# Row maxima of the verdict, gate weights and filler matmuls of the front put at other places in the engines' orders of a gated recurrence with a dense mixture of experts

## The chip, the cores and the metric

The kernel runs on one core of one Trainium2 chip. That core has TensorE (PE in the profile, its weight loads PEld), VectorE (DVE), ScalarE (ACT), GpSimd (POOL), SyncE (SP, which here only issues DMAs) and 16 DMA engines. Each engine runs its own list of instructions in order and waits at an instruction until what it needs is there. The metric is the time of one execution in microseconds (us).

## The reference

Two stages. A gated linear recurrence in each of 4 x 8 heads makes x, 3072 tokens by 384; a dense mixture of 8 experts (384 to 1024 to 384) is applied to x, each expert's result weighted with a column of P, which eight rounds of row and column normalization (Sinkhorn) make from the gate's logits.

```
f = 1 / (1 + exp(-f_logit))
for t in range(S):                       # S = 768, head_dim 48
    state = f[t] * state + outer(k[t], v[t])
    y[t] = q[t] @ state
x = y as (3072, 384)
P = exp(x @ w_gate - max); 8 x: P /= P.sum(1); P /= P.sum(0); P *= N / E
out = sum over e of P[:, e] * (relu(x @ w1[e]) @ w2[e])
```

## The kernel before

All values are float32. A product is made from float16 pairs: each operand is split into a high and a low part (names ending in h and l: ACT makes the high part, DVE the low one as the difference), and TensorE adds three products, hh, hl and lh.

**The front and the items.** The recurrence is cut into 24 items. An item loads q, k and f as one tile (q_1 for item 1; its DMA is line 493) and v (vr, line 498). ACT makes the gates ft (line 502), DVE scans them (r, line 507, then pi, its reciprocal, and the scaled q), splits keys and queries (kb line 551, ql line 554), TensorE transposes the keys (ktp, drained by ACT into kt, line 533), makes the scores (aps, masked by DVE as am, line 571) and the block states (kvps; u, st and sl on DVE, lines 582, 583 and 593), and then the item's result (yps of the item), which ACT and DVE drain as xh (line 616) and xl (line 619). Then the gate of an item, `gate` at line 472, multiplies x by the gate weights wgs into lps. The first three items are written as `early_item` (line 487), the others as `item`. Each is a generator that is moved on by one step per turn of the loop at lines 895 to 911; g counts the turns.

**Filler.** While items run, the first two experts are already computed on the tokens that are ready. `moe_tile` (line 404) does one expert on 128 tokens: 36 + 36 first-layer matmuls (hps, made into hh and hl), then 24 second-layer matmuls (yps_0_0 for the first tile), drained by ACT into yr_0_0 and stored. `fill` (line 845) issues as many matmuls of this filler per turn as the table FILL (line 80) gives credits: an entry (g, n) gives n credits from turn g on; a first-layer matmul of the first tiles costs a third of a credit, a second-layer one a whole.

**Loads.** `load` (line 335) brings a quarter of an expert's w1 or w2: a DMA into w1r or w2r, then ACT makes w1h or w2h (line 347), then DVE w1l or w2l (line 349), each at its own step. `first` is the list of the eight loads of expert 0 (four w1, then four w2). `gate_weights` (line 313) has the DMA of wgr and, one step later, one ACT and one DVE instruction that make wgs. `at_steps` puts a step of such a load into a turn.

**Order.** `mm` (line 278) hangs every matmul behind the one written before it, and `pin` (line 270) does the same for an engine's other instructions; so the order in the code is the order on TensorE, ACT, DVE and POOL. All matmuls have line 279 in the profile. DMAs are issued on SP.

**The second stage.** 48 periods (`period`, line 1198) do the other six experts on larger tiles. Each has 15 slots of six first-layer matmuls (kb_A to kb_F, drained by ACT and DVE), and between them the second-layer matmuls of the period before (`layer2`, line 1066): groups of twelve into a PSUM tile kyps, which is added to acc by DVE (line 1089) or by ACT (yt, line 1092) and POOL. The pool `psm` that kyps comes from has two buffers. In some of the last periods a chain of checks runs at given slots. Its end is `verdict` (line 799), which brings five columns of 128 numbers down to one number each: `partition_reduce` (line 94) transposes a column on TensorE into a tile gd_t of the same pool `psm`, and DVE reduces the row (gd_r, line 99). Between the two is a `yield`, so that the reduce comes in the chain's next slot. The numbers only decide whether a general path is used instead, which these inputs don't take.

## Time and profile before

| | |
|---|---|
| median of 3 runs | 1570.53 us (1569.91 to 1571.93) |
| profiled execution | 1571.4 us |
| its span, first to last instruction | 1569.7 us |
| mean granted TensorE clock | 0.994 |
| moved by DMA | 114.39 MB, 73 GB/s |

The profile is one execution. Busy times are sums over instructions; the chain that ended last is followed back from the last instruction through what released each. A wait is put down to the instruction that came last. In rows of the timeline the first two numbers are the start and the length in us, and what is in brackets is the idle time just ahead on that engine and what ended it.

### The profile page before, as it was taken

What the parts mean: (1) busy time and instruction counts of PE and PEld (TensorE: products, weight loads), DVE (VectorE), ACT (ScalarE), POOL (GpSimd) and SP (SyncE); (2) the same over time, 40 slices, a digit from 0 to 9 for tenths busy, and PEclk for the clock granted to TensorE, in tenths of its full rate; (3) what the DMA queues carried; (4) which work ended last, traced back from release to release, by engine and by line L of the source; (5) the groups of instructions that cost most, each with busy time, mean ns of one, the idle gap of its engine ahead of it and who ended that gap; (6) DMA issues with size and microseconds to landing.
All of it is one profiled execution on the core that took longest, in us unless ns stands there. A gap on an engine that the chain in (4) does not pass through costs nothing.

```text
span 1569.7 us, 32490 instructions
## 1 busy us (share of the span) xinstructions
PE 1527.5 (97%) x13462; PEld 1108.9 (71%) x13462; DVE 1095.0 (70%) x1810; ACT 778.2 (50%) x1489; POOL 515.2 (33%) x656
## 2 busy tenths in 40 slices
PE   7799999999999999999999999999999999999998
PEld 4588887666555777777777777777777777776675
DVE  7878888895776766676767677666666666755554
ACT  5555556553333655555455554445444445444432
POOL 1144444453529112333333332223322223222211
PEclk8999999999999999999999999999999999999999
DMA  8265445541001222232322222121212111100011
GB/s 254 74 147 140 121 121 132 135 116 35 20 27 50 67 63 79 66 92 66 91 66 84 74 86 62 47 65 42 68 44 63 42 43 51 32 11 11 6 51 69
DMA packets 89678, 114.39 MB, mean 73 GB/s; under 512 B 50640, under 2 KB 67152, under 8 KB 89520
## 3 DMA queue, kind: packets, MB, share of 16 engines
q1 hardware_dynamic: 89520, 112.22, 25.5%
q8 instruction: 107, 1.75, 0.5%
q14 instruction: 51, 0.42, 0.1%
HBM read 88.41 MB, written 14.16 MB: 65 GB/s over the span
## 4 chain that ended last, share of the span: by engine, by line
PE 89%; DVE 5%; ACT 2%; DMA 1%; POOL 1%; issue 1%; SPq 0%; ACTq 0%; DVEq 0%; POOLq 0%
PE kyps L279 35%; PE yps L279 12%; PE hps L279 10%; PE kb_B L279 8%; PE kb_A L279 8%; PE kb_D L279 6%; PE kb_C L279 4%; PE kb_E L279 2%; PE kb_F L279 2%; PE kvps L279 1%; PE aps L279 1%; DMA q<-in_qkf_dram 1%; POOL xs L936 1%; DVE hl L381 1%; DMA w1r<-in_w_dram 0%
## 5 line engine op out<-in xcount | busy, mean ns | idle before, releaser
L1093 POOL TENSOR_TENSOR acc<-acc,yt 128x384 f32<-128x384 f32 x172 | 173.3, 1008 | 638.0 <-ACT yt L1092 638.0
L279 PE MATMUL kyps<-k2h,kh 128*128 128x384 f16 x1152 | 375.5, 326 | 5.8 <-ACT yt L1092 2.1
L279 PE MATMUL kyps<-k2l,kh 128*128 128x384 f16 x1152 | 375.5, 326 | 0.0
L279 PE MATMUL kyps<-k2h,kl 128*128 128x384 f16 x1152 | 375.5, 326 | 0.0
L279 PEld LDWEIGHTS <-k1h 128*128 128x128 f16 x2880 | 281.5, 98 | 70.5
L279 PEld LDWEIGHTS <-kh 128*128 128x128 f16 x2304 | 225.4, 98 | 103.8
L1092 ACT ACTIVATE yt<-kyps,pes 128x384 f32<-128x384 f32 x172 | 100.1, 582 | 325.8 <-PE kyps L279 323.9
L279 PEld LDWEIGHTS <-k1l 128*128 128x128 f16 x1440 | 140.7, 98 | 63.2 <-issue 7.5
L1089 DVE SCALAR_TENSOR_TENSOR acc<-kyps,pes,acc 128x384 f32<-128x384 f32 x92 | 56.8, 618 | 175.3 <-PE kyps L279 175.3
L279 PEld LDWEIGHTS <-kl 128*128 128x128 f16 x1152 | 112.7, 98 | 53.1 <-issue 9.0
L279 PE MATMUL yps<-w2h,hl 128*128 128x384 f16 x384 | 125.9, 328 | 4.5 <-DVE hl L428 4.5
L1186 ACT ACTIVATE cp<-kb_A 128x512 f32<-128x512 f32 x144 | 86.3, 599 | 85.6 <-PE kb_A L279 85.0
L279 PE MATMUL yps<-w2l,hh 128*128 128x384 f16 x384 | 125.9, 328 | 1.5 <-DVE w2l L349 1.5
L279 PE MATMUL yps<-w2h,hh 128*128 128x384 f16 x384 | 125.7, 327 | 0.2 <-DVE hl L381 0.2
L279 PEld LDWEIGHTS <-w1h 128*128 128x128 f16 x1344 | 99.5, 100 | 33.9 <-issue 3.0
L1186 ACT ACTIVATE cp<-kb_B 128x512 f32<-128x512 f32 x144 | 87.2, 605 | 52.6 <-DVE kb_B L1188 51.0
L1191 DVE TENSOR_TENSOR cp<-kb_D,cp 128x512 f32<-128x512 f32 x144 | 98.8, 686 | 16.2 <-PE kb_D L279 15.3
L279 PEld LDWEIGHTS <-hh 128*128 128x128 f16 x768 | 74.8, 99 | 47.1 <-issue 2.6
L279 PE MATMUL hps<-xl,w1h 128*128 128x128 f16 (+1 forms) x672 | 86.0, 260 | 1.5 <-DVE xl L619 1.1
L279 PE MATMUL hps<-xh,w1h 128*128 128x128 f16 (+1 forms) x672 | 85.1, 260 | 0.5 <-DVE hl L381 0.4
L279 PE MATMUL hps<-xh,w1l 128*128 128x128 f16 (+1 forms) x672 | 85.1, 260 | 0.0
L279 PE MATMUL kb_A<-xbh,k1h 128*128 128x256 f16 x288 | 78.5, 273 | 0.2 <-ACT cp L1186 0.2
(243 smaller groups left out, 3616.6 us busy)
## 6 DMA issues: line engine op xcount, KB each, us to landing
wm<-in_w_dram SPq DMA_DIRECT2D x64, 384.0 KB, 3.0
q<-in_qkf_dram SPq DMA_DIRECT2D x23, 672.0 KB, 5.2
vr<-in_vbd_dram SPq DMA_DIRECT2D x24, 384.0 KB, 3.5
ys<-yr SPq DMA_DIRECT2D x48, 192.0 KB, 2.3
k1r<-in_w_dram SPq DMA_DIRECT2D x24, 384.0 KB, 3.0
k2r<-in_w_dram SPq DMA_DIRECT2D x24, 384.0 KB, 3.1
yb<-ys SPq DMA_DIRECT2D x48, 192.0 KB, 2.4
out_dram<-acc SPq DMA_DIRECT2D x24, 192.0 KB, 1.9
```

Of the source, the lines that this page charges most:

```text
L279: ins = (nc.tensor.transpose if transpose else nc.tensor.matmul)(**kw)
L381: held[0] = pin(nc.vector.scalar_tensor_tensor(out=tl, in0=ps, scalar=0.0, in1=th, op0=ALU.max, op1=ALU.subtract))
L936: pin(nc.gpsimd.tensor_tensor(out=block(r), in0=block(p), in1=block(q), op=ALU.add if op == '+' else ALU.subtract))
L1089: pin(nc.vector.scalar_tensor_tensor(out=y, in0=ps, scalar=p, in1=y, op0=ALU.mult, op1=ALU.add))
L1092: pin(nc.scalar.activation(out=yt, in_=ps, func=AF.Copy, scale=p))
L1093: pin(nc.gpsimd.tensor_tensor(out=y, in0=y, in1=yt, op=ALU.add))
L1186: pin(nc.scalar.activation(out=fresh(ev[2]), in_=bk, func=AF.Copy))
L1191: pin(nc.vector.tensor_tensor(out=fresh(ev[4]), in0=bk, in1=old, op=ALU.add if ev[2] == '+' else ALU.subtract))
```

## The change

Two parts.

1. `partition_reduce` has no `yield` any more: the row's reduce is issued right behind its transpose, in the same slot; `verdict` then yields twice after each column, so that the transposes stay in their slots.
2. In the front, the credits of turns 4 to 7 are spread: six second-layer matmuls of the first tile in each of turns 5, 7, 8 and 10. The DMA of wgr is issued ahead of those of w1r, and wgs is made ahead of the first xh. The four loads of w2r are issued behind item 1's q and v. w1h_2 is made behind the first xh, w1l_2 ahead of item 1's r, and the w2h and w2l come later.

```diff
-FILL = ((0, 12), (1, 8), (2, 4), (3, 0), (4, 6), (8, 0), (12, 4.7), (22, 8.7), (43, 8.2))
+FILL = ((0, 12), (1, 8), (2, 4), (3, 0), (5, 6), (6, 0), (7, 6), (9, 0), (10, 6), (11, 0), (12, 4.7), (22, 8.7), (43, 8.2))
...
     row = pool.tile([1, 1], F32, name=name + "_r")
-    yield
     pin(nc.vector.tensor_reduce(out=row, in_=ps[0:1, :], axis=AX.X, op=op))
     return row
...
         for n, (col, op) in enumerate(((5, ALU.min), (4, ALU.max), (2, ALU.max), (6, ALU.min), (0, ALU.min))):
-            rows.append((yield from partition_reduce(nc, cst, psm, "m", identf, g[:, col:col + 1], op, f"gd{n}", mm, pin)))
+            rows.append(partition_reduce(nc, cst, psm, "m", identf, g[:, col:col + 1], op, f"gd{n}", mm, pin))
+            yield
             yield
...
     wgen = gate_weights()
     it = early_item(0)
     go(it)
-    for gen in first:
+    go(wgen)
+    for gen in first[:4]:
         go(gen)
     nxt = early_item(1)
     go(nxt)
-    go(wgen)
+    for gen in first[4:]:
+        go(gen)
     go(it, 8)
     go(first[0])
     go(it, 2)
     go(first[1])
     go(it)
     go(first[0])
+    go(wgen)
+    go(it)
     go(it)
     go(first[2])
-    go(it)
     go(first[3])
     go(it)
     go(nxt)
     go(first[1])
+    go(first[2])
     live, g = [it, nxt], 0
     for n in range(2, 8):
-        at_steps(first[n], *((n - 2,) if n < 4 else (n - 2, n - 1)))
-    at_steps(wgen, 11)
+        at_steps(first[n], *((0,), (1,), (2, 3), (3, 5), (5, 7), (6, 10))[n - 2])
```

What this moves on the engines is shown at three places. Lines of the changed kernel are one lower than before up to the loop and three higher behind it. A row has line, operation, what is written, what is read and the shape; the number at the end of a name tells one tile from another.

SP at the start of the program, before: the loads behind item 0's.

```order
L498 DMA vr_161<-in_vbd_dram 128x768
L343 DMA w1r_0_163<-in_w_dram 128x768
L343 DMA w1r_1_165<-in_w_dram 128x768
L343 DMA w1r_2_167<-in_w_dram 128x768
L343 DMA w1r_3_169<-in_w_dram 128x768
L343 DMA w2r_0_171<-in_w_dram 128x768
L343 DMA w2r_1_173<-in_w_dram 128x768
L343 DMA w2r_2_175<-in_w_dram 128x768
L343 DMA w2r_3_177<-in_w_dram 128x768
L493 DMA q_1_179<-in_qkf_dram 112x1536
L498 DMA vr_181<-in_vbd_dram 128x768
L315 DMA wgr<-in_wg_dram 128x384
```

The same place in the changed kernel:

```order
L497 DMA vr_161<-in_vbd_dram 128x768
L314 DMA wgr<-in_wg_dram 128x384
L342 DMA w1r_0_165<-in_w_dram 128x768
L342 DMA w1r_1_167<-in_w_dram 128x768
L342 DMA w1r_2_169<-in_w_dram 128x768
L342 DMA w1r_3_171<-in_w_dram 128x768
L492 DMA q_1_173<-in_qkf_dram 112x1536
L497 DMA vr_175<-in_vbd_dram 128x768
L342 DMA w2r_0_177<-in_w_dram 128x768
L342 DMA w2r_1_179<-in_w_dram 128x768
L342 DMA w2r_2_181<-in_w_dram 128x768
L342 DMA w2r_3_183<-in_w_dram 128x768
```

q_1 and vr of item 1 have gone ahead of the four w2r, and wgr ahead of everything but item 0's own loads.

DVE in the front, before: item 1 from its split of the keys (kb) to its masked scores (am) and its first state (u), and then to the last piece before xl.

```order
L551 TENSOR_TENSOR kb_125<-q_1_179,kb_125 48x8x64 x2
L349 SCALAR_TENSOR_TENSOR w2l_1_510<-w2r_1_173,w2h_1_509 128x768
L554 TENSOR_TENSOR ql_499<-q_1_179,qh_498 112x512
L349 SCALAR_TENSOR_TENSOR w2l_2_520<-w2r_2_175,w2h_2_519 128x768
L564 SCALAR_TENSOR_TENSOR vl_139<-vr_181,vh_133 128x768
L349 SCALAR_TENSOR_TENSOR w2l_3_565<-w2r_3_177,w2h_3_564 128x768
L571 SCALAR_TENSOR_TENSOR am_589<-aps_538,mask 128x512
L582 TENSOR_TENSOR u_1_618<-kvps_0_594,st_576 112x384
```

In the changed kernel:

```order
L550 TENSOR_TENSOR kb_125<-q_1_173,kb_125 48x8x64 x2
L553 TENSOR_TENSOR ql_501<-q_1_173,qh_500 112x512
L348 SCALAR_TENSOR_TENSOR w2l_1_512<-w2r_1_179,w2h_1_511 128x768
L563 SCALAR_TENSOR_TENSOR vl_139<-vr_175,vh_133 128x768
L570 SCALAR_TENSOR_TENSOR am_577<-aps_529,mask 128x512
L348 SCALAR_TENSOR_TENSOR w2l_2_556<-w2r_2_181,w2h_2_555 128x768
L581 TENSOR_TENSOR u_1_604<-kvps_0_582,st_568 112x384
```

w2l_1 stands behind ql now, w2l_2 behind am, and w2l_3 has left this place: it comes behind item 2's r, pi and reciprocal, ahead of the carry. On TensorE the first six second-layer matmuls, which stood ahead of ktp_1_0, stand behind aps; only these six are ahead of kvps_0, where eighteen were; and the last six stand behind item 1's own yps and a wps.

DVE in the second stage, before: the slots at and behind the first of the five transposes (acc is the add of a kyps group, kb_A to kb_D are drains of the first layer).

```order
L1188 TENSOR_TENSOR kb_A<-kb_A,cp_13_19170 128x512
L1089 SCALAR_TENSOR_TENSOR acc_8534<-kyps_0_1_19178,pes,acc_8534 128x384
L994 SCALAR_TENSOR_TENSOR k1l_2_18993<-k1s_2_18900,k1h_2_18992 128x640 x2
L1188 TENSOR_TENSOR kb_B<-kb_B,cp_0_19231 128x512
L1089 SCALAR_TENSOR_TENSOR acc_8534<-kyps_1_0_19220,pes,acc_8534 128x384
L994 SCALAR_TENSOR_TENSOR k1l_2_18993<-k1r_2_18865,k1h_2_18992 128x256
L994 SCALAR_TENSOR_TENSOR k1l_2_18993<-k1r_2_18865,k1h_2_18992 128x384
L1188 TENSOR_TENSOR kb_C<-kb_C,cp_9_19260 128x512
L1191 TENSOR_TENSOR cp_2_19277<-kb_D,cp_6_19203 128x512
L1196 SCALAR_TENSOR_TENSOR kl_0_0_19119<-kb_A,kh_0_0_19118 128x512
L1188 TENSOR_TENSOR kb_D<-kb_D,cp_7_19294 128x512
L99 TENSOR_REDUCE gd_r<-gd_t 1x1
```

In the changed kernel:

```order
L1191 TENSOR_TENSOR kb_A<-kb_A,cp_13_19170 128x512
L98 TENSOR_REDUCE gd_r<-gd_t 1x1
L1092 SCALAR_TENSOR_TENSOR acc_8534<-kyps_0_1_19178,pes,acc_8534 128x384
L997 SCALAR_TENSOR_TENSOR k1l_2_18993<-k1s_2_18900,k1h_2_18992 128x640 x2
L1191 TENSOR_TENSOR kb_B<-kb_B,cp_0_19232 128x512
```

The reduce has moved up by ten instructions, from behind the drain of kb_D to just behind that of kb_A. The other four move in the same way.

## The prediction

> **What bounds the kernel now.** I read the page's shares first, then the list of waits on TensorE, then the stretches in which those waits lie.

> ```profile
> PE 1527.5 (97%) x13462; PEld 1108.9 (71%) x13462; DVE 1095.0 (70%) x1810; ACT 778.2 (50%) x1489; POOL 515.2 (33%) x656
> PE 89%; DVE 5%; ACT 2%; DMA 1%; POOL 1%; issue 1%; SPq 0%; ACTq 0%; DVEq 0%; POOLq 0%
> ```

> TensorE is busy for 97% of the span and carries 89% of the chain that ends last. No matmul is removed, so only time in which TensorE waits can be won. The list of waits on TensorE (engine and line waited for, us in total, times, longest) has these entries where the change works:

> ```profile
> PE lps L279 <- DVE wgs L318: 3.3, 1, 3.3
> PE aps L279 <- DVE ql L554: 2.9, 2, 1.6
> PE kvps L279 <- ACT kt L533: 2.4, 1, 2.4
> PE kyps L279 <- ACT yt L1092: 2.1, 3, 0.7
> PE kyps L279 <- DVE acc L1089: 2.1, 3, 0.7
> PE yps L279 <- DVE w2l L349: 1.5, 1, 1.5
> PE ktp L279 <- DVE kb L551: 0.5, 1, 0.5
> ```

> They lie in two places: the front (before 55 us: wgs, ql, kt, w2l, kb) and the five periods of the second stage in which the verdict transposes a column (acc, yt).

> **The verdict.** Six successive periods, one undisturbed and then the five with a transpose (start:end, length, busy time of PE, PEld, DVE, ACT, POOL, granted clock, DMA share, GB/s):

> ```profile
> 1368.19:1389.79 21.60, 21.60 (x164) 15.84 (x162) 13.44 (x35) 10.89 (x21) 8.26 (x14) 1.00 0.04 13
> 1389.79:1412.74 22.95, 22.11 (x165) 15.91 (x163) 13.83 (x24) 9.12 (x17) 3.99 (x4) 1.00 0.07 18
> 1412.74:1436.42 23.68, 22.22 (x166) 15.91 (x164) 12.52 (x22) 11.81 (x22) 8.24 (x14) 1.00 0.06 18
> 1436.42:1459.96 23.54, 22.18 (x164) 15.91 (x163) 14.79 (x27) 10.06 (x18) 3.99 (x4) 1.00 0.00 1
> 1459.96:1483.70 23.74, 22.40 (x165) 15.90 (x163) 11.85 (x22) 9.33 (x17) 3.98 (x4) 1.00 0.01 1
> 1483.70:1506.65 22.95, 22.11 (x165) 15.91 (x163) 11.06 (x19) 9.11 (x17) 4.00 (x4) 1.00 0.12 42
> ```

> The five are 22.95 + 23.68 + 23.54 + 23.74 + 22.95 = 116.86 us long, where five of the undisturbed length are 108.00: an excess of 8.86 us. Its cause stands in the rows of the transposed column and its reduce, and in TensorE's timeline:

> ```profile
> L279 PE MATMUL gd_t<-identf,wg x5: 272/272/273, 1394.7 to 1488.6; 128*1 128x128 f32 x5
> L99 DVE TENSOR_REDUCE gd_r<-gd_t x5: 267/268/269, 1407.3 to 1501.2; 1x1 f32<-1x128 f32 x5
> ...
> 1401.04 0.33 PE L279 MATMUL kyps<-k2l,kh 128*128 128x384 f16 x1
> 1402.08 0.32 PE L279 MATMUL kyps<-k2h,kh 128*128 128x384 f16 x1 [0.71 <-DVE acc L1089]
> ```

> The first column is transposed at 1394.7 and reduced at 1407.3. For 12.6 us, over half a period, it holds one of the pool's two PSUM buffers, and the groups of second-layer matmuls (kyps) share the other: each can begin only when the group before has been drained by its add. The timeline shows one such start, 1.04 us behind the matmul before it, though nothing else stood between.

> The change puts the reduce into the slot of the transpose. DVE is busy for 11 to 15 us of these periods, so it has room, and no instruction is added: a reduce of 0.27 us stands earlier. The buffer is then free long before the next group asks for it, as in the undisturbed period. What stays is the five transposes themselves on TensorE: between nothing (hidden) and their 0.272 us each (1.36 in all); two matmuls of 256 columns in the neighbourhood are 0.11 us apart, and I take that, 5 × 0.11 = 0.55. **The verdict's term is −(8.86 − 0.55) = −8.3 us**, between −7.5 and −8.86. The new cost, DVE waiting at the reduce for the transpose with the add of a kyps group behind it, is at least nothing and at most a transpose and a reduce, 0.54 us each time; it is DVE's and not TensorE's time, and DVE's idle hours cover it (22.95 − 13.83 = 9.1 us in the first of the periods), so I take nothing. If that cover were gone, 5 × 0.54 = 2.7 us would come back.

> **The front.** From lps on (the gate of item 0) all engines have the same order in both kernels, so the term of the front is how much earlier the first-layer matmuls of item 1's tile begin, just behind lps. They stand here now, with the instructions that lead there (start, us, engine, line, operation, idle time before it and what ended it):

> ```profile
> 5.05 3.76 SPq L343 DMA_DIRECT2D w2r<-in_w_dram  x4
> 10.44 0.33 SPq L498 DMA_DIRECT2D vr<-in_vbd_dram  x1
> ...
> vr<-in_vbd_dram SPq DMA_DIRECT2D x3, 384.0 KB, 12.4
> ...
> 17.07 0.85 ACT L347 ACTIVATE w1h<-w1r 128x768 f16<-128x768 f32 x1
> 21.20 0.62 ACT L502 ACTIVATE ft<-q 112x504 f32<-112x504 f32 x1 [3.29 <-DMA q<-in_qkf_dram]
> 40.31 0.49 ACT L442 ACTIVATE yr<-yps 128x384 f32<-128x384 f32 x1 [2.23 <-PE yps L279]
> 43.02 1.32 ACT L616 ACTIVATE xh<-yps 96x384 f16<-96x384 f32 x4 [0.62 <-PE yps L279]
> 46.53 0.53 ACT L317 ACTIVATE wgs<-wgr 128x384 f16<-128x384 f32 x1
> ...
> 18.60 0.96 DVE L349 SCALAR_TENSOR_TENSOR w1l<-w1r,w1h 128x768 f16<-128x768 f32 x1
> 21.86 1.23 DVE L507 TENSOR_TENSOR_SCAN r<-ft,ind 112x512 f32<-112x512 f32 x1 [2.31 <-ACT ft L502]
> 28.76 0.69 DVE L428 SCALAR_TENSOR_TENSOR hl<-hps,hh 128x512 f16<-128x512 f32 x1 [0.61 <-ACT hh L427]
> 33.52 0.69 DVE L554 TENSOR_TENSOR ql<-q,qh 112x512 f16<-112x512 f32 x1
> 35.86 0.95 DVE L349 SCALAR_TENSOR_TENSOR w2l<-w2r,w2h 128x768 f16<-128x768 f32 x1
> 36.72 0.69 DVE L571 SCALAR_TENSOR_TENSOR am<-aps,mask 128x512 f32<-128x512 f32 x1
> 39.41 0.56 DVE L582 TENSOR_TENSOR u<-kvps,st 112x384 f32<-112x384 f32 x1 [1.99 <-PE kvps L279]
> 41.56 0.96 DVE L593 SCALAR_TENSOR_TENSOR sl<-st,sh 112x768 f16<-112x768 f32 x1 [0.41 <-ACT sh L587]
> 44.02 0.51 DVE L544 TENSOR_TENSOR carry<-kvps,st 112x384 f32<-112x384 f32 x1
> ...
> 47.33 0.25 PE L279 MATMUL lps<-wgs,xh 128*128 128x16 f16 x3 [3.28 <-DVE wgs L318]
> 47.52 1.44 PE L279 MATMUL hps<-xh,w1h 128*128 128x128 f16 x12
> ```

> A w2l takes 35.86 to 36.72 = 0.86 us of DVE, and I use 0.87. I walk down this list with the new order.

> *Loads.* q_1 now goes ahead of the four w2r instead of behind them, so ft no longer waits 3.29 us for it; what ends last then is ACT's w1h work. With w1h_2 now behind the first xh, two w1h stand before ft: 17.07 + 2 × 0.79 = 18.65 instead of 21.20. The price is on the w2r. The last of the loads, vr_1, landed at 10.44 + 12.4 = 22.8; the same set now ends with w2r_3, behind one more load, wgr. So w2r_3 lands near 23.7 and w2r_0 before that; ACT asks for w2h_0 near 24.5. I cost it at nothing; each us later than that would cost up to one.

> *DVE to ql.* r comes behind two w1l: 18.60 + 2 × 0.87 = 20.35, 1.5 us earlier. kt, kvps, hps and hh follow ft (2.55 us earlier) and I let them move by 2.4, a little less, since TensorE has item 0's matmuls to end first; hl, which waits for hh, is at 26.35 (−2.4). From hl to ql DVE needed 33.52 − 28.76 = 4.76 us. In it w2l_1 (0.87) and an idle 0.43 before it go, since w2l_1 now stands behind ql: 3.45 remain, and ql starts at 29.8 (−3.7).

> *am, u, sl.* Between ql and am DVE has now w2l_1 and vl, not three pieces of w2l and vl: am at 29.8 + 0.6 + 2 × 0.87 = 32.15 (−4.6). u waited 1.99 us because twelve second-layer matmuls stood ahead of kvps_0 on TensorE at half rate. Now six stand there: aps ends near 31.2, six by 0.16 to 0.32 are 1 to 1.9 us, kvps takes 0.7, so it is ready at 32.9 to 33.8, while DVE is free at 32.15 + 0.61 + 0.87 = 33.65. I take u at 33.8 (−5.6) and sl, the same 2.15 us behind, at 35.95, ending at 36.9 (−5.6).

> *What is late next.* Item 1's yps could be drained into xh at about 37.4. But the last six second-layer matmuls need w2l_3, which now stands behind r, pi and the reciprocal on DVE, and yr_0_0 stands ahead of xh on ACT. From sl's start to the carry were 44.02 − 41.56 = 2.46 us, so w2l_3 runs from 38.4 to 39.3, the six matmuls end at 40.3, yr takes 0.4 and 0.5 us with its start, and xh runs from 40.85 to 42.15. Some 3.4 us of the gain are given back here. The wait for wgs, 3.28 us, is gone: its ACT instruction (0.53 us) now lies in ACT's wait for the first xh, and its DVE one ahead of the first xl. Were it not hidden there, ft would end at 18.65 + 0.53 + 0.62 = 19.8, still ahead of r at 20.35.

> So hps begins at 42.25 instead of 47.52: **the front's term is −5.3 us.** All listed stalls of the front together, 3.28 + 1.6 + 2.43 + 1.5 + 0.5 = 9.3 us, are its upper end; the lower end is nothing, if DVE's work after it swallows what is won.

> Against the profiled execution (span 1569.7 us, run 1571.4) the sum is −8.3 − 5.3 = −13.6, or 1557.8. Its run lies 0.9 us above the median of 1570.53; I give the forecast against the median: **1556.9 us.**

> One more thing speaks for caution, the clock that TensorE was granted in two stretches of the front (columns as above):

> ```profile
> 28.40:35.20 6.80, 3.24 (x40) 1.86 (x39) 6.00 (x9) 5.37 (x10) 0.38 (x1) 1.00 0.44 137
> 35.20:38.60 3.40, 3.40 (x14) 1.75 (x12) 2.21 (x3) 0.63 (x1) 0.00 (x0) 0.50 0.97 305
> ```

> Behind 6.8 us in which TensorE was busy for 3.24, the next 3.4 us ran at half rate. The change takes the second-layer matmuls out of the wait for kb: from the end of wps (25 to 27) to kb's end at 29.8 TensorE has nothing to do. A stretch of 3.4 us at half rate costs at most 1.7 us.

> [...]

> **The rivals.** 0.2% of this kernel, 3.1 us, is about what a measurement of it can tell from no change.

> - *One more stretch at half clock* in the front, as above, with no other one saved: 1556.9 + 1.7 = 1558.6. For it speaks the new wait; against it that the kernel already ran at half rate in 35.2 to 38.6 and would only exchange one such stretch for another.
> - *The front gives nothing*: DVE is the bound there, and what TensorE no longer waits for at lps it waits for later: 1570.5 − 8.3 = 1562.2. Against it: DVE's own instructions ahead of lps end five us earlier too.
> - *The front gives all its stalls*: 1570.5 − 8.3 − 9.3 = 1552.9. Against it: the 3.4 us given back at yr.
> - *The verdict gives nothing*: the buffers do not alternate again, because the reduce still ends too late for the group that wants its buffer. 1570.5 − 5.3 = 1565.2. Against it: the reduce is now 0.3 us behind the transpose, and a slot is 21.60 / 15 = 1.44 us.
> - *It does not do what it says*, each wait being replaced by one of equal length: 1570.5.
> - *Slower*: the w2r land late. On ACT w2h_0 stands ahead of hh_0_0_1, qh and vh, so each us past 24.5 delays item 1 by one. The verdict's 8.3 and the front's 5.3 cover 13.6 us; to be slower by 3.1 it needs 16.7 us, a landing after 41 us, while the whole set ended at 22.8; 1574 at that point.

> **How the numbers follow.** The forecast of 1556.9 has 0.55; half clock (1558.6) 0.15; front nothing (1562.2) 0.10; front all (1552.9) 0.08; verdict nothing (1565.2) 0.07; no effect (1570.5) 0.03; slower (1574) 0.02. Faster by over 0.2% hold all but the last two: 0.95, within 0.2% 0.03, slower 0.02. The range runs from all stalls of the front, 1552.9, to none of them, 1562.3.

> **What would show it.** In the profile after: the five periods with a transpose at about 21.7 us each, reduces within a us of their transposes, no wait of kyps on acc or yt there; ft at 18.6, ql at 29.8, sl at 36, yr just ahead of xh at 40.9, no wait for wgs, lps near 42.2. I would be wrong if ft still waited for q_1, if ACT waited for w2r, if the periods kept over 22.5 us, or if the time from lps to the second stage grew by what the front won.

## The result, and the profile after

| | before | changed |
|---|---|---|
| median | 1571.10 us (4 runs, 1569.91 to 1571.93) | 1560.88 us (4 runs, 1560.01 to 1561.55) |
| span of the profiled execution | 1569.7 us | 1558.3 us |

The ratio is 0.9935, with a 95% interval from 0.9918 to 0.9952: 10.2 us less, where 13.6 were forecast. The two profiled executions lie further apart than the medians, 1571.4 − 1560.0 = 11.4 us, since that of the changed kernel was the fastest of its four.

TensorE's list of waits in the changed kernel (engine, line waited for, us in total, times, longest) has lost wgs, and of kyps yt, acc and gd_r (1.0 us before: there TensorE waited for the reduce itself). kt and w2l have shrunk to 0.2. The wait for hl is the same in both kernels, the one for ql is shorter (2.9 before) and the one for kb longer (0.5 before); those for w1l and xh and the one of kb_A are new:

```profile
PE ktp L278 <- DVE kb L550: 4.5, 2, 3.7
PE yps L278 <- DVE hl L427: 4.5, 3, 3.1
PE aps L278 <- DVE ql L553: 2.1, 1, 2.1
PE hps L278 <- DVE w1l L348: 1.5, 1, 1.5
PE hps L278 <- ACT xh L615: 1.1, 1, 1.1
PE kb_A L278 <- ACT yr L397: 0.6, 1, 0.6
```

**The verdict.** Of the five periods with a transpose (columns as in the prediction) the first two and the last, and the instructions of the transposed column:

```profile
1387.23:1408.93 21.70, 21.70 (x164) 15.92 (x163) 13.98 (x24) 9.10 (x17) 3.99 (x4) 1.00 0.07 19
1408.93:1430.74 21.81, 21.81 (x165) 15.92 (x163) 12.69 (x23) 11.72 (x22) 8.24 (x14) 1.00 0.06 17
...
1474.21:1495.91 21.70, 21.70 (x164) 15.92 (x163) 11.16 (x19) 9.10 (x17) 4.00 (x4) 1.00 0.12 45
...
L278 PE MATMUL gd_t<-identf,wg x5: 272/273/273, 1392.1 to 1479.1; 128*1 128x128 f32 x5
L98 DVE TENSOR_REDUCE gd_r<-gd_t x5: 277/278/278, 1392.4 to 1479.4; 1x1 f32<-1x128 f32 x5
  PE gd_t L278: 3.5, 4
```

From 1387.23 to 1495.91 are 108.68 us, 0.68 more than five undisturbed periods instead of 8.86. The reduce starts 0.3 us behind its transpose, and TensorE is busy for the whole of each period. The last line is what DVE now pays: it stood idle before the reduces for 3.5 us in all, four times, until the transpose came. TensorE does not wait for it.

**The front.** DVE, ACT and TensorE at the places that the prediction walked down (start, us, engine, line, operation, and in brackets the idle time before it):

```profile
18.30 0.61 ACT L501 ACTIVATE ft<-q 112x504 f32<-112x504 f32 x1
40.93 0.49 ACT L441 ACTIVATE yr<-yps 128x384 f32<-128x384 f32 x1 [3.44 <-PE yps L278]
41.31 1.34 ACT L615 ACTIVATE xh<-yps 96x384 f16<-96x384 f32 x4
...
20.09 1.22 DVE L506 TENSOR_TENSOR_SCAN r<-ft,ind 112x512 f32<-112x512 f32 x1
29.32 0.69 DVE L553 TENSOR_TENSOR ql<-q,qh 112x512 f16<-112x512 f32 x1
31.67 0.69 DVE L570 SCALAR_TENSOR_TENSOR am<-aps,mask 128x512 f32<-128x512 f32 x1
34.54 0.56 DVE L581 TENSOR_TENSOR u<-kvps,st 112x384 f32<-112x384 f32 x1 [1.32 <-PE kvps L278]
39.12 0.91 DVE L348 SCALAR_TENSOR_TENSOR w2l<-w2r,w2h 128x768 f16<-128x768 f32 x1
42.68 1.49 DVE L618 SCALAR_TENSOR_TENSOR xl<-yps,xh 96x384 f16<-96x384 f32 x4 [1.59 <-ACT xh L615]
49.39 0.68 DVE L553 TENSOR_TENSOR ql<-q,qh 112x512 f16<-112x512 f32 x1
...
40.73 0.22 PE L278 MATMUL lps<-wgs,xh 128*128 128x16 f16 x3
42.12 1.30 PE L278 MATMUL hps<-xh,w1h 128*128 128x128 f16 x12 [1.09 <-ACT xh L615]
```

The first hps of item 1 starts at 42.12 us; 42.25 was forecast. So close a match is in part luck: xh came 0.46 us later than forecast, but the first hps did not wait for its end at 42.65. And behind hps the gain melts. These rows of the kernel before answer to DVE's last xl and ql (item 2's) above and to the first matmul of the second stage, with that matmul in the changed kernel under them:

```profile
47.19 1.48 DVE L619 SCALAR_TENSOR_TENSOR xl<-yps,xh 96x384 f16<-96x384 f32 x4
54.08 0.68 DVE L554 TENSOR_TENSOR ql<-q,qh 112x512 f16<-112x512 f32 x1
...
511.12 0.27 PE L279 MATMUL kb_A<-xbh,k1h 128*128 128x256 f16 x1
...
508.69 0.27 PE L278 MATMUL kb_A<-xbh,k1h 128*128 128x256 f16 x1 [0.63 <-ACT yr L397]
```

Earlier than before: 47.52 − 42.12 = 5.40 us at hps, 54.08 − 49.39 = 4.69 at ql, and 511.12 − 508.69 = 2.43 at the second stage.

### The profile page after: what moved, and what is told of

The parts are those of the page before. It is cut to its first block, busy times and chain, and to the rows that moved or that the text cites. A ratio compares the mean times of both kernels' runs of the same rounds, so it can differ in the third digit from the quotient of the medians.

```text
span 1558.3 us, 32489 instructions
## 1 busy us (share of the span) xinstructions
PE 1522.9 (98%) x13462; PEld 1106.3 (71%) x13462; DVE 1095.3 (70%) x1810; ACT 776.4 (50%) x1489; POOL 515.1 (33%) x656
## 3 DMA queue, kind: packets, MB, share of 16 engines
q8 instruction: 107, 1.75, 0.5%
## 4 chain that ended last, share of the span: by engine, by line
PE 90%; DVE 6%; ACT 2%; POOL 1%; issue 1%; ACTq 0%; DVEq 0%; POOLq 0%
PE kyps L278 36%; PE yps L278 12%; PE hps L278 9%; PE kb_A L278 8%; PE kb_B L278 8%; PE kb_D L278 6%; PE kb_C L278 4%; PE kb_E L278 2%; PE kb_F L278 2%; PE kvps L278 1%; PE aps L278 1%; POOL xs L939 1%; PE wps L278 1%; DVE hl L380 1%; DVE w2l L348 0%
## 5 line engine op out<-in xcount | busy, mean ns | idle before, releaser
L1092 DVE SCALAR_TENSOR_TENSOR acc<-kyps,pes,acc 128x384 f32<-128x384 f32 x92 | 56.9, 618 | 172.0 <-PE kyps L278 172.0
L278 PEld LDWEIGHTS <-hh 128*128 128x128 f16 x768 | 75.2, 99 | 46.4 <-issue 2.3
L1194 DVE TENSOR_TENSOR cp<-kb_D,cp 128x512 f32<-128x512 f32 x144 | 98.9, 687 | 12.8 <-PE kb_D L278 11.8
## 6 DMA issues: line engine op xcount, KB each, us to landing
wm<-in_w_dram SPq DMA_DIRECT2D x64, 384.0 KB, 3.0
vr<-in_vbd_dram SPq DMA_DIRECT2D x24, 384.0 KB, 3.4
k1r<-in_w_dram SPq DMA_DIRECT2D x24, 384.0 KB, 3.1
k2r<-in_w_dram SPq DMA_DIRECT2D x24, 384.0 KB, 3.0
```

Source lines behind the costliest of these rows:

```text
L278: ins = (nc.tensor.transpose if transpose else nc.tensor.matmul)(**kw)
L1092: pin(nc.vector.scalar_tensor_tensor(out=y, in0=ps, scalar=p, in1=y, op0=ALU.mult, op1=ALU.add))
L1194: pin(nc.vector.tensor_tensor(out=fresh(ev[4]), in0=bk, in1=old, op=ALU.add if ev[2] == '+' else ALU.subtract))
```

## Where the front's gain went: three theories

*DVE.* Only 4.69 of the 5.40 pass ql of item 2. The way there leads over DVE's xl, which began at 47.19 before, behind wgs, and waits now until 42.68 for the end of xh: 4.5 us earlier and not 5.4.

*The clock.* TensorE is idle for 3.1 us in both kernels, waiting for hl. In the two traces the granted clock changes at 21.55, 28.37, 35.20, 38.61, 45.44 and 52.27 us (before) and at 28.03, 34.86, 72.41 and 75.82 (changed), in each of them whole multiples of 3.41 us apart. Four windows, two of the changed kernel and then two of the one before, laid along that grid (columns as above; the seventh figure, 1.00 or 0.50, is the clock):

```profile
69.00:72.40 3.40, 0.70 (x5) 0.20 (x2) 3.40 (x4) 1.20 (x2) 2.99 (x2) 1.00 0.31 104
72.40:75.80 3.40, 3.02 (x10) 1.49 (x11) 3.11 (x3) 0.00 (x0) 3.25 (x3) 0.50 0.58 145
...
72.70:76.10 3.40, 1.69 (x11) 0.78 (x8) 3.40 (x4) 1.34 (x3) 2.00 (x2) 1.00 0.08 10
76.10:79.60 3.50, 2.14 (x18) 1.43 (x19) 3.50 (x4) 0.65 (x2) 3.42 (x2) 1.00 0.70 215
```

In the changed kernel the idle time fell into one window, TensorE was busy for 0.70 of 3.40 us, and the next window ran at half rate. In the kernel before the same idle time lay across an edge, 1.69 and 2.14 us busy, and the clock stayed. Ten second-layer matmuls are slower for it (0.26 to 0.32 us from one to the next, 0.16 ahead of the wait), and the lead of 4.7 us is 3.2 behind them.

*A PSUM bank.* kb_A waits 0.63 us for the last drain of the front (yr, line 397). No engine's order differs there. By the theory, the last tile of the front lies in another PSUM bank: the pool `psn` has two, and they have changed places. The bank numbers are those of the built programs and stand in no trace; the trace shows only for which drain kb_A waits.

| | bank of the last yps | of the one before it in `psn` | of kb_A | kb_A waits for the drain of |
|---|---|---|---|---|
| before | 3 | 2 | 2 | the one before |
| changed | 2 | 3 | 2 | the last |

Why they changed places is not shown: the other turn of yps_0_0 alone does not settle it, since in warm_front below, where yps_0_0 keeps that turn, kb_A waits for no drain.

The rival to all three was that the gain holds and only the executions differ.

## The experiments

Each kernel was run in three rounds against the kernel before; medians are given. For all of them I also read how much earlier than in the profiled execution of the kernel before the same instruction of DVE starts, at five places: al of item 0 (13.9 us before), ql of item 2 (54.1), and the first instructions behind 100, 1350 and 1520 us. Each kernel has one profile. The median of the kernel before moves by 1.0 us between the sets of runs, so medians of different sets are compared by how far each lies below its own "before".

| kernel | median, us | before in its runs | al | ql | 100 | 1350 | 1520 |
|---|---|---|---|---|---|---|---|
| changed | 1560.88 | 1571.10 | 0.17 | 4.69 | 3.20 | 2.56 | 10.74 |
| verdict_only | 1562.45 | 1571.10 | 0.75 | 1.54 | 1.54 | 1.70 | 9.88 |
| front_only | 1569.80 | 1571.10 | 0.11 | 4.65 | 3.14 | 2.62 | 2.64 |
| bank_swap | 1560.42 | 1571.10 | 0.94 | 5.57 | 2.78 | 3.05 | 11.24 |
| yr_late | 1560.67 | 1571.10 | −0.50 | 5.86 | 3.16 | 2.67 | 10.86 |
| warm_gap | 1560.43 | 1570.09 | −0.63 | 3.88 | 1.90 | 1.14 | 9.31 |
| warm_front | 1557.99 | 1570.09 | −0.60 | 5.34 | 5.34 | 5.60 | 13.78 |
| all_four | 1555.57 | 1570.09 | 0.64 | 8.40 | 7.39 | 7.70 | 15.88 |
| wgen_only | 1570.59 | 1570.09 | −0.20 | 1.79 | −0.76 | −0.53 | −0.49 |
| before_warm | 1570.00 | 1571.02 | 0.87 | 0.86 | −0.18 | 0.12 | 0.14 |
| after_warm | 1557.18 | 1571.02 | 0.24 | 6.18 | 6.18 | 6.31 | 14.49 |
| all_five | 1555.15 | 1571.02 | −0.41 | 7.35 | 7.34 | 7.60 | 15.79 |

### One part of the change at a time

verdict_only is the kernel before with this edit alone; front_only is the changed kernel with the edit undone.

```diff
     row = pool.tile([1, 1], F32, name=name + "_r")
-    yield
...
-            rows.append((yield from partition_reduce(...)))
+            rows.append(partition_reduce(...))
+            yield
             yield
```

> The kernel before with the verdict's part alone. By the theory that the two parts are independent and the verdict is worth its 8.3 us: 1571.1 - 8.3 = 1562.8 us, the five periods 21.7 us each, the front as before. By the rival that part of the 8.2 us in the changed kernel came from the changed order of the buffers in the front: 1 us or more less than that, 1564 or later.

> The changed kernel with the verdict as before. By the theory that of the 5.4 us won at the first hps of item 1 only 2.4 reach the second stage (0.7 lost to DVE's order, 1.4 to a stretch at half clock near 72 us, 0.8 to kb_A's wait for the last drain at 508 us): 1568.7 us, the second stage from about 520.5 where a stretch at half rate falls on 72 to 76, and 519 where it does not. By the rival that the front's 5.3 hold to the end: 1565.8.

verdict_only came to 1562.45 (ratio 0.994, 0.992 to 0.996), front_only to 1569.8 (0.9991, 0.9982 to 1.0001: not told apart from no change). 8.65 and 1.3 us add up to 9.95 of the 10.2, as independent parts would; the interval of the first alone reaches from 6.3 to 12.6 us, so the table is the better witness. There the verdict is worth 1520 minus 1350, and that is 8.17 to 8.19 in all nine kernels that have it, whatever their front, and 0.02 to 0.04 in the three that do not. front_only's profile repeats the changed kernel's: 4.65, then 3.14, then 2.62. Its time of 1569.8 is 1.1 above what I expected. The 2.4 were read from one pair of profiles, and the execution of the kernel before in it was a late one: in verdict_only, whose front is the one of before, ql stands 1.54 earlier. Against verdict_only's profile the lead of front_only at 1350 us is 2.62 − 1.70 = 0.9 us. The first kb_A of front_only stands at 508.75 us; no row shown here answers to the 520.5 and 519 of the expectation.

### The bank

```diff
-        return (psn if n % 2 and not late else psm).tile(shape, F32, name=name, tag="m")
+        return (psn if n % 2 and not late and name != "yps_1_7_2" else psm).tile(shape, F32, name=name, tag="m")
```

> The changed kernel, with the last second-layer group ahead of the second stage put into the other pool's bank, so that the first kb_A takes a bank that was drained long ago. By the theory that kb_A waits because the two banks of the front changed places: the wait of 0.6 us of kb_A on yr is gone and the kernel is 0.8 us faster than the changed one, 1560.1 against 1560.9. By the rival that the wait comes from ACT being late and not from the bank: no change in that wait.

The last yps and the first kb_A on TensorE in bank_swap:

```profile
508.15 0.33 PE L278 MATMUL yps<-w2l,hh 128*128 128x384 f16 x1
508.31 0.27 PE L278 MATMUL kb_A<-xbh,k1h 128*128 128x256 f16 x1
```

kb_A follows 0.16 us behind, the distance of these matmuls from each other, with no wait. From 100 to 1350 the lead grows by 0.27 us here and shrinks by 0.64 in the changed kernel: 0.9 us by the bank alone. The other kernels agree: in the four in which kb_A waits 0.6 us for yr (changed, front_only, yr_late, warm_gap) the lead shrinks by 0.49 to 0.76 us from 100 to 1350, and in the eight in which it does not the lead grows by 0.13 to 0.31. The medians, 1560.42 and 1560.88, show half of it; in the profiled execution two windows from 70.9 to 77.7 us ran at half rate (5.57 at ql, 2.78 at 100). That ACT was late as such is excluded: the edit moves one tile to the other pool and leaves ACT's order as it was, and the wait is gone.

### yr behind xh

```diff
-... (9, 0), (10, 6), (11, 0), (12, 4.7), ...
+... (9, 0), (11, 6), (12, 4.7), ...
```

> The changed kernel with yr_0_0 behind item 1's xh and kb on ACT; nothing else moves. By the theory that yr ahead of xh gives back part of the front's gain: xh at 38.5 instead of 41.3, xl at 41.0 instead of 42.7 (then DVE is what ends last), hps of item 1 at 40.9 instead of 42.1, ql of item 2 1.5 us earlier; 1 to 1.5 us faster than the changed kernel where the clock's stretches stay. By the rival that DVE or the clock takes it back by 80 us: no change in the time, 1560.9.

```profile
39.49 1.35 ACT L615 ACTIVATE xh<-yps 96x384 f16<-96x384 f32 x4 [1.34 <-PE yps L278]
41.66 1.49 DVE L618 SCALAR_TENSOR_TENSOR xl<-yps,xh 96x384 f16<-96x384 f32 x4
48.22 0.68 DVE L553 TENSOR_TENSOR ql<-q,qh 112x512 f16<-112x512 f32 x1
```

This execution began 0.67 us later than the changed kernel's (al at −0.50 against 0.17). Measured from there, ql came 6.36 us earlier instead of 4.52: 1.84 were won, and DVE no longer waited at xl. But at 100 us 3.16 were left: this time two windows, 49.9 to 53.3 and 73.7 to 77.2, ran at half rate. The time, 1560.67, is that of the changed kernel. The theory was right up to ql, and the rival that the clock takes it back about the time.

### TensorE kept busy

A `wps` is a matmul of 512 columns on constants whose result nobody reads; the kernel has some of them already. warm_front puts thirteen more into item 1's wait for kb (first edit), warm_gap ten into the wait for hl (second edit).

```diff
-        warm(3 if i else 5)
+        warm((5, 16, 3)[i])
...
             for a, b in ((hh, wh), (hl, wh), (hh, wl)):
+                if (e, u, t, n) == (0, 0, 2, 13):
+                    wk = psa.tile([128, 512], F32, name="wk", tag="a", bufs=1)
+                    for _ in range(10):
+                        mm(out=wk, lhsT=ind[:, 0:128], rhs=ind[:, 0:NB * C], start=True, stop=True)
```

> The changed kernel with ten matmuls of 512 columns on constants, whose result nobody reads, put on TensorE ahead of the second-layer matmul that waits 3.08 us for hl at 69.7 us; everything else keeps its order. By the theory that this idle gap, when it fills one window of the clock's grid, brings the 3.4 us at half rate behind it: no stretch at 0.50 between 69 and 80 us, the shift against before stays 4.7 us instead of falling to 3.2, time 1.4 us less than the changed kernel's, 1559.5. By the rival that the half rate there has another cause or costs nothing: 1560.9, and the ten matmuls cost nothing either.

> The changed kernel with thirteen more such matmuls on TensorE in item 1's wait for kb (24.9 to 29.3 us). They also turn the order of the two banks back, so kb_A waits for no drain: 0.8 us by that alone. By the theory that the idle wait makes the half rate at 28 to 35 us, and that this lies on the path (kvps late for u): no stretch at 0.50 there, u at 33.2 instead of 34.5, hps of item 1 at 40.8 instead of 42.1; up to 2.1 us less than the changed kernel, 1558.8. By the rival that the half rate there is covered by DVE: 0.8 us less, 1560.1.

warm_gap alone is undecided: 1558.31 to 1562.25 in four runs. In its profiled execution, the slowest, the gap at 70 us brought no half rate any more, but an earlier one did:

```profile
46.70:50.10 3.40, 1.39 (x21) 1.11 (x20) 2.14 (x4) 2.83 (x5) 0.00 (x0) 1.00 0.01 2
50.10:53.50 3.40, 2.57 (x36) 2.57 (x36) 2.34 (x4) 0.41 (x1) 0.00 (x0) 0.50 0.48 130
53.50:57.00 3.50, 3.50 (x33) 3.16 (x31) 0.00 (x0) 2.19 (x4) 0.00 (x0) 0.51 0.68 187
```

warm_front came to 1557.99 (0.9924, 0.9907 to 0.994). That is 0.8 below the expected 1558.8 as it stands, but its own "before" was faster too: it lies 12.1 us below that, the changed kernel 10.2 below its own, and 1.9 more is near the 2.1 expected. The same stretch in the changed kernel, and then in warm_front, with u in warm_front:

```profile
24.60:28.00 3.40, 1.00 (x7) 0.39 (x7) 3.11 (x5) 2.04 (x4) 1.57 (x1) 1.00 1.03 398
28.00:31.40 3.40, 1.99 (x29) 1.83 (x30) 3.36 (x6) 3.15 (x6) 0.00 (x0) 0.51 0.78 186
31.40:34.90 3.50, 3.50 (x22) 2.27 (x20) 2.18 (x4) 1.68 (x4) 0.00 (x0) 0.51 0.91 249
...
26.20:29.60 3.40, 2.97 (x14) 1.18 (x12) 3.10 (x6) 2.04 (x4) 0.73 (x1) 1.00 0.73 280
29.60:33.00 3.40, 2.60 (x45) 2.15 (x46) 3.37 (x5) 3.33 (x7) 0.00 (x0) 1.00 0.78 199
33.00:36.40 3.40, 3.40 (x59) 2.62 (x58) 3.00 (x6) 2.04 (x6) 0.00 (x0) 1.00 0.97 314
...
33.90 0.55 DVE L581 TENSOR_TENSOR u<-kvps,st 112x384 f32<-112x384 f32 x1
```

The wait for kb had left TensorE busy for 1.00 of 3.40 us, and aps, six second-layer matmuls and kvps ran at half rate behind it. With the window filled they run at full rate and u no longer waits for kvps. Counted from al, ql gains 5.34 + 0.60 = 5.94 against the changed kernel's 4.52: 1.4 us, where 1.3 were expected at hps. No window between ql and 100 us ran at half rate, though nothing was put into the gap at 70 us: in this execution an edge fell into the gap, with 1.95 and 1.77 of 3.40 us busy in the windows on either side (67.1 to 73.9 us), which is luck. The 5.34 us reach the second stage whole.

> The kernel before with matmuls on constants, whose result nobody reads, in two idle stretches of TensorE: twelve ahead of lps (the wait for wgs, 44 to 47.3 us) and ten in the wait for hl at 74.4 us. If the half rate behind those waits lies on the path of the kernel before as it does in the changed one: 1 to 2 us less, about 1569. If only the changed kernel loses by the clock: 1570.5.

> The changed kernel with the warm matmuls in the wait for kb and in the wait for hl; yr_0_0 stays ahead of xh. Its banks stand so that kb_A waits for no drain. By the theory that, with the clock held up and the bank out of the way, the front is worth the 4.7 us that it has at item 2's ql and the verdict 8.2: 12.9 below the kernel before with its own warm matmuls, about 1556.5 against 1569. By the rival that the front is worth its 5.3 at the first hps: 13.6 below. By the rival that the front is worth little however the clock stands: 9 to 10 below.

before_warm is the kernel before with the ten matmuls at hl and twelve more ahead of lps; after_warm is the changed kernel with both of the places above.

```diff
-        warm(2 if i else 4)
+        warm((4, 14, 2)[i])
```

They came to 1570.0 and 1557.18, 12.8 us apart: the theory of 4.7 and 8.2 had 12.9, its rivals 13.6 and 9 to 10. But the theory's 4.7 is not what their two profiles show: at ql they stand 6.18 − 0.86 = 5.3 us apart, at 1350 6.2. So the match of the medians is in part luck. Each of the two stands away from its own forecast, 1569 and 1556.5, by 1.0 and 0.7: before_warm kept one window at half rate, 53.9 to 57.3, and lost there the 1.0 that it shows between ql and 100.

With these kernels the clock's part can be counted over all twelve, by the granted clock of each trace:

| windows at half rate between ql of item 2 and 80 us | kernels | lead lost from ql to 100 us |
|---|---|---|
| none | verdict_only, warm_front, after_warm, all_five | −0.01 to 0.01 |
| one | changed, front_only, all_four, before_warm | 1.01 to 1.51 |
| two | bank_swap, yr_late, warm_gap, wgen_only | 1.98 to 2.79 |

The kernel before has none there in its own profile.

### Together

all_four has both warm places, yr late and the other bank; all_five has eight more `wps` in item 2's wait for ql.

```diff
         transposed(1, 0)
-        if not i:
-            warm(2)
+        if i != 1:
+            warm(8 if i else 2)
```

> The changed kernel with the warm matmuls of both places, yr_0_0 behind xh and kb, and the last group of second-layer matmuls in the other bank. If the front's gain is lost to the clock, to yr and to the bank as the theory has it: 1.4 + 1.3 + 1.2 + 0.8 = 4.7 us less than the changed kernel, 1556.2. If the half rate only comes at another gap of the front: 1559 to 1560.

> The kernel with warm matmuls at two places, late yr and the other bank, and eight more such matmuls in item 2's wait for ql (44.5 to 46.4 us). If that wait of 1.95 us makes the half rate that its profile showed from 47.6 to 51.0: no stretch at 0.50 between 8 and 110 us, 1 to 1.7 us less, about 1554.3. If DVE covers that stretch: 1555.6, as without them.

all_four came to 1555.57 us (0.9904, 0.9887 to 0.992), all_five to 1555.15 (0.9901, 0.9883 to 0.9919): both beat both kernels. Counted from al, ql has 8.40 − 0.64 = 7.76 and 7.35 + 0.41 = 7.76. That is the sum of the parts, 4.52 for the changed kernel, 1.42 for the warm front and 1.84 for yr, 7.78. all_four loses 1.0 by 100 us in a window at half rate (47.6 to 51.0), all_five nothing; its clock stood at full from 8.7 us to 1551. Its median is lower by 0.4 us, where 1 to 1.7 were expected; against their own "before" the two lie 15.9 and 14.5 us lower, which is 1.35 apart. The two intervals don't part them, so the times leave this open.

### The gate weights alone

wgen_only is the kernel before with this:

```diff
+    go(wgen)
     for gen in first:
         go(gen)
     nxt = early_item(1)
     go(nxt)
-    go(wgen)
...
     go(first[0])
+    go(wgen)
     go(it)
...
-    at_steps(wgen, 11)
```

> The kernel before with one part of the front's change alone: the DMA of wgr ahead of w1r's, and the two instructions that make wgs in the wait for the first xh. The wait of 3.3 us on wgs goes. By the theory that DVE sets what is left: xl behind the scaled q at 45.1 instead of 47.2, hps of item 1 at 44.4 instead of 47.5, 2.1 us faster at item 2's ql and so 1569.0, plus or minus a stretch of the clock (1.7). By the rival that the wait is worth what the list says: 3.3 us, 1567.8. By the other rival that the time is set elsewhere: 1571.1.

It came to 1570.59 us (ratio 1.000, 0.999 to 1.001). The wait of 3.3 us, the longest of the front, was gone: lps stood at 44.44 us instead of 47.33, and ql 1.8 us earlier. Two windows then took it all:

```profile
49.30:52.70 3.40, 0.89 (x15) 0.62 (x13) 2.14 (x4) 2.76 (x5) 0.00 (x0) 1.00 0.01 2
52.70:56.10 3.40, 3.08 (x41) 3.08 (x41) 1.83 (x3) 0.92 (x2) 0.00 (x0) 0.50 0.62 177
73.20:76.60 3.40, 0.32 (x3) 0.04 (x2) 3.40 (x4) 0.79 (x2) 3.40 (x2) 0.99 0.38 116
76.60:80.00 3.40, 3.40 (x11) 1.60 (x12) 2.69 (x2) 0.00 (x0) 3.22 (x3) 0.50 0.72 203
```

In this execution the whole idle time before hl fell into one window, as in the changed kernel. The DVE theory was right up to ql, and the rival that the time is set elsewhere was right about the sum.

## Why the prediction came out as it did

The time lies in the range, but only the verdict's term makes it so. The front's term, −5.3, came to 1.3 us in front_only and to 2.4 at the second stage in the pair of profiles, and the range had room for all of that, since it ran down to no gain from the front. That the time falls inside it is in this part luck. 1560.9 is nearer to the rival "the front gives nothing" (1562.2) than to the forecast (1556.9).

*The verdict, −8.3: right.* 8.18 in every kernel that has it. The transposes left 0.68 us, where 0.55 was taken. DVE's new wait exists (3.5 us) and is covered, as forecast.

*The walk through the front: right to half a us up to am.* ft 18.30 (18.65 forecast), r 20.09 (20.35), ql 29.32 (29.8), am 31.67 (32.15). u came at 34.54 instead of 33.8: the clock was at half rate for the whole of aps, the six matmuls and kvps, where I had taken the upper end for the six alone. xh and hps at 41.31 and 42.12 (40.85, 42.25). The w2r were in time: ACT makes w2h at 24.48 without a wait for a DMA. Of the 3.4 us that yr was to give back, yr_late shows 2.5 at xh (39.49 less its later start of 0.67, against 41.31) and 1.84 at ql.

*Wrong: "From lps on … all engines have the same order in both kernels, so the term of the front is how much earlier the first-layer matmuls of item 1's tile begin".* The same order does not make the same length. Three things lie between. DVE's xl and ql moved by 4.5 and 4.7 and not by 5.4. The clock took 1.5 us in this execution and 0 to 2.8 in the others, by the number of windows at half rate that fell between ql and 80 us. And a tile in another bank, which no row of an order shows, took 0.9. The prediction had one more window at half rate as a rival (1558.6), in the front ahead of hps; windows at half rate were there, at 28 to 35 us, but the one that cost the lead behind ql lay at 72 us, where the prediction looked at nothing. Nor is the count of such windows the cost: the kernel before has five of 3.4 us in the front (21.5 to 28.4, 35.2 to 38.6 and 45.4 to 52.3 us, of which the prediction showed one), the changed kernel three. Those five all lie ahead of item 2's ql; of the changed kernel's three one lies behind it.

*The profiled execution of before* was taken as typical to 0.9 us. For the front it was not: the same front stood 1.54 us earlier at ql in verdict_only. Item 0's al alone stands anywhere from 12.97 us (bank_swap) to 14.54 (warm_gap), and the traces show why. In all thirteen profiles TensorE's first `wps` begins at 2.98 us, and these matmuls follow each other by 0.43 us until the clock comes to full, by 0.22 us from then on. That moment lies between 6.0 us (bank_swap) and 9.2 (warm_gap), at 7.9 in the kernel before and 7.6 in the changed one, and the later it is, the later is al, in the same order in all thirteen. So the front's worth in the changed kernel is nearer to the 1.3 us of front_only (its interval reaches from 0 to 2.8) than to the 2.4 of one pair of profiles; it is not told apart from nothing by the times.

The rivals: that the verdict gives nothing is excluded, and so is that the front gives all its stalls. That the front gives nothing is not excluded by the times; the reason given for it, "DVE is the bound there", covers only the 0.7 us lost ahead of ql.

Left open: how the grid of the clock's windows comes to lie where it does at the start of an execution. No run here set it.

## What to carry to other kernels

A gain at one instruction is worth what is left of it at the next place where all engines are bound again; follow it there, instruction by instruction, before calling it a term of a sum. Where matmuls come in bursts with waits of 2 to 4 us between them, as here, read the granted clock behind each wait. In this kernel, with the wait of 2.4 us on kt gone and one of 3.7 us on kb in its place, the first stretch of half clock came at 28.0 to 34.9 us instead of 21.5 to 28.4, and a few matmuls on constants in a wait were worth more than taking a wait away: thirteen of them gave 1.4 us at ql, and taking away the wait of 3.3 us on wgs gave nothing in the time. And when tiles change their turn in a rotating pool, look at which buffer the next stage's first tile will take.

## What the runs showed of the hardware

```profile
39.80:43.20 3.40, 1.95 (x22) 1.26 (x21) 1.77 (x5) 2.81 (x7) 1.14 (x1) 1.00 0.55 174
43.20:46.70 3.50, 3.38 (x23) 2.47 (x23) 3.37 (x7) 1.13 (x3) 0.00 (x0) 0.51 0.00 0
...
70.50:73.90 3.40, 1.77 (x11) 1.09 (x12) 3.40 (x4) 0.63 (x1) 3.33 (x3) 1.00 0.77 225
73.90:77.30 3.40, 3.40 (x63) 3.37 (x61) 1.50 (x2) 1.65 (x4) 1.57 (x2) 1.00 0.81 202
```

The grid lay elsewhere from execution to execution: with the same front, the windows at half rate began at 21.5, 35.2 and 45.4 us in the kernel before and at 30.3 and 43.9 in verdict_only, and from 21.5 to 30.3 are 8.8 us, no multiple of 3.41.
